# Retention attention beside a swish MoE on one core: pairs of attention chunks replaced by single chunks, one PSUM bank re-labelled

## The chip, the cores and the metric

The kernel runs on one core of a Trainium2 chip. The metric is the device time of one execution in microseconds (us); before the change it was 314.33 us, the median of 3 runs (313.99 to 314.72).

## What is computed

The reference, cut to what matters (8 batches, 8 heads, 576 positions, head size 64; model width 512, hidden width 2048):

```python
scores = scale * np.matmul(q, k.transpose(0, 1, 3, 2))
gamma = 1.0 - 2.0 ** (-5.0 - np.arange(H, dtype=np.float32))
rel = pos[:, None] - pos[None, :]
Dmat = np.where(rel >= 0, gamma[:, None, None] ** rel[None, :, :], 0.0)
attn_out = np.matmul(scores * Dmat[None], v)
x = attn_out.transpose(0, 2, 1, 3).reshape(B * S, H * D)      # 4608 x 512
h = x @ w_in                                                  # 4608 x 2048
out = (h * sigmoid(beta * h)) @ w_out                         # 4608 x 512
```

Since the decay is a power of a position difference, the kernel scales q rows by gamma^i and v rows by gamma^-j, so that the decay mask becomes a plain 0/1 causal mask.

## The kernel before

**The work.** Of each batch, positions 0 to 511 are cut into four chunks of 128 (c = 0 to 3), and the 64 positions left over of two batches make one tail chunk (four in all). The list seq (lines 51 to 55) gives their order; the two tails of four batches stand side by side after batch 3 and after batch 7. For each chunk the kernel does these steps:

- load_q, load_kv, load_tail (lines 73 to 103): loads, issued by SyncE (the SP queue).
- pre_q, pre (lines 232 to 266): GpSimd (POOL) scales q into qs and v into vn and casts k into kn.
- kT and qT, the transposes. For batches 0 to 2 they are done by TensorE (PE) into PSUM (t_q, t_k, lines 284 to 295) and copied out by ScalarE (ACT) or VectorE (DVE). From batch 3 on (XB = 3) they are DMA transposes that ACT issues (x_q, x_k, x_tail, lines 271 to 282).
- a_sc (line 304): 8 matmuls for the scores, each using 64 of the 128 rows of the array (the profile's form 64*128), then DVE multiplies two halves by the mask into R (line 324).
- a_O (line 345): 8 matmuls R times v, each filling 64 of the 128 columns (form 128*64).
- a_cross (line 326): 4 matmuls (8 half-size ones for a tail) that add what earlier chunks of the batch contribute through the running state; full array. Chunk 0 has none.
- a_x (line 362): the chunk's output is copied from PSUM to xT, by DVE for chunks 8 and later.
- a_st (line 375): 4 matmuls that add the chunk to the state; full array; ACT copies the state out in two halves (line 390). Tails have none.

**The order.** The program is written in the order in which each engine runs it (manual schedule). MoE work is a list called fill, of which one element, here called a filler, is four matmuls of 512 columns: up (line 395) makes one of 16 hidden slices of a block of 512 rows, and ACT applies silu from PSUM into gT; down (line 408) makes a quarter of an output tile, and after each fourth one DVE copies it out and SP stores it. Blocks come in the order 0 to 6, tails, 7. Fillers 0 to 15 are up of block 0, 16 to 31 down of block 0, 32 to 51 up of block 1, 52 to 67 down of block 1, 68 to 83 up of block 2, 84 to 99 down of block 2, and so on by 32. Each attention step has a filler number, and merged (line 432) puts it ahead of that filler in the program. So a step's number fixes its place in every engine's queue: PE, DVE, ACT, POOL and SP each work through their own part in order, and wait there for what they need.

Chunks 0 to 3 are done ahead of the fillers (lines 446 to 483). Chunks 4 to 7 have fractional numbers written out by hand (lines 517 to 520). From chunk 8 (E = 8) on, pair_steps (line 534) handles two chunks i and i+1 in two visits, five fillers apart:

```python
def first(i):  a_st(i); a_sc(i); a_sc(i + 1)
def second(i):
    for f in (a_O, lambda j: a_cross(j, False), a_x):
        f(i); f(i + 1)
    a_st(i + 1)
```

Loads, casts and transposes of a pair stand a fixed number of fillers ahead of its first visit. Lines 553 to 563 spread 14 pairs over the blocks.

**Buffers.** PSUM has eight banks here: tag mm 3 (fillers, and the second half of t_q), sc 2 (scores), O 2 (outputs, the scores of the second chunk of a pair, and the PE transposes), st 1 (state). In the on-chip memory there are 4 kn and 4 kT buffers, 6 vn, 6 for loaded k and v, 2 for loaded q; loaded tails share the q buffers.

Of the kernel before, what the change touches and what calls it, by code (L numbers as in the profile page):

```python
# [19 lines left out]
def kernel(  # L20
# [30 lines left out]
    seq = []  # L51
    for b in range(B):
        seq += [(b, c) for c in range(CB)]
        if b % CB == CB - 1:
            seq += [(None, b // 2 - 1), (None, b // 2)]
    full = [i for i, (b, _) in enumerate(seq) if b is not None]

    consts = ctx.enter_context(tc.tile_pool(name="consts", bufs=1))
# [8 lines left out]

    NQ = 6
    E = 2 * CB
    XB = 3  # L70
    q_tiles, kv_tiles = {}, {}

# [23 lines left out]
    def load_tail(t):  # L96
        if t >= NT:
            return
        tl = stage.tile([P, 4, H, D], F32, name="tln", tag="qn", bufs=2)
        for j, src in enumerate((q, k, v)):  # L100
            for x in range(2):
                nc.sync.dma_start(tl[x * TL:(x + 1) * TL, j], src[2 * t + x, :, MB:, :].rearrange("h s d -> s h d"))
        tail_tiles[t] = tl
# [142 lines left out]
    def pre(i):  # L246

        b, c = seq[i]
        vn = sb.tile([P, H, D], BF16, name="vn", tag="vn", bufs=6)
        if b is None:  # L250
            t = tail_tiles.pop(c)
            qk = sb.tile([P, 2, H, D], BF16, name="kn", tag="kn", bufs=4)
            qkT = sb.tile([P, 2, HP, P], BF16, name="kT", tag="kT", bufs=4)
            nc.gpsimd.tensor_tensor(qk[:, 0], t[:, 0], gains(gq, CB), ALU.mult)
            nc.gpsimd.tensor_copy(qk[:, 1], t[:, 1])
            nc.gpsimd.tensor_tensor(vn[:], t[:, 2], gains(gv, CB), ALU.mult)
            live[i] = dict(qk=qk, qkT=qkT, kT=qkT[:, 1], vn=vn)
            return
        if c % 2 == 0:
            pair[b, c // 2] = (sb.tile([P, 2, H, D], BF16, name="kn", tag="kn", bufs=4),  # L260
                               sb.tile([P, 2, HP, P], BF16, name="kT", tag="kT", bufs=4))
        t = kv_tiles.pop(i)
        kn, kT = pair[b, c // 2]
        live[i] = dict(kn=kn[:, c % 2], kT=kT[:, c % 2], vn=vn)
        nc.gpsimd.tensor_copy(kn[:, c % 2], t[:, 0])  # L265
        nc.gpsimd.tensor_tensor(vn[:], t[:, 1], gains(gv, c), ALU.mult)  # L266
# [15 lines left out]
        turn(live[i]["qkT"], live[i]["qk"])  # L282

    def t_q(b, u):
        T = psum.tile([P, CB, 2, P], BF16, name="T", tag="mm" if u else "O", bufs=3 if u else 2)
        for i in range(CB):
            for p in range(2):
                nc.tensor.transpose(T[:, i, p, :], heads(batch[b]["qs"][:, i], 2 * u + p), ident[:])  # L288
        (nc.vector.tensor_copy if u else nc.scalar.copy)(batch[b]["qT"][:, :, 2 * u:2 * u + 2], T[:])

    def t_k(i):
        T = psum.tile([P, HP, P], BF16, name="T", tag="O", bufs=2)
        for p in range(HP):
            nc.tensor.transpose(T[:, p, :], heads(live[i]["kn"], p), ident[:])  # L294
        nc.scalar.copy(live[i]["kT"], T[:])  # L295

# [7 lines left out]
    def a_sc(i):  # L304
        L = live[i]
        L["R"] = R = sb.tile([P, 2, HP, P], BF16, name="R", tag="R", bufs=2)

        tag = "O" if i >= E and (i - E) % 2 else "sc"
        sc = [psum.tile([P, HP, P], F32, name="sc", tag=tag, bufs=2) for _ in range(2)]
        for p in range(HP):  # L310
            for j in range(2):
                r = slice(j * D, (j + 1) * D)
                rhs, view = q_cols(i, r, p)
                nc.tensor.matmul(view(sc[j][:, p, :]), L["kT"][r, p, :], rhs, start=True, stop=True,  # L314
                                 skip_group_check=True)
        mask = causal if seq[i][0] is not None else causal2
        m_b = mask[:].unsqueeze(1).to_broadcast([P, HP, P])
        if i == CB - 1:

            half = sb.tile([P, HP, P], BF16, name="half", tag="half", bufs=1)  # L320
            nc.scalar.copy(half[:], sc[1][:])
            sc[1] = half
        for j in range(2):
            nc.vector.tensor_tensor(R[:, j], sc[j][:], causal4[:] if i == CB - 1 else m_b, ALU.mult)  # L324

    def a_cross(i, first):

        b, c = seq[i]
        L = live[i]
        if first:  # L330
            L["O"] = psum.tile([P, HP, P], F32, name="O", tag="O", bufs=2)
        if c == 0 and b is not None:
            return
        for p in range(HP):
            rhs, view = q_cols(i, slice(0, P), p)
            if b is None:
                for x in range(2):
                    r = slice(x * TL, (x + 1) * TL)
                    nc.tensor.matmul(L["O"][:, p, r], ends[(2 * c + x) % 4][:, p, :], rhs[:, r],  # L339
                                     start=False, stop=True, skip_group_check=True)  # L340
            else:
                nc.tensor.matmul(view(L["O"][:, p, :]), sbds[(c - 1) % NS][:, p, :], rhs,  # L342
                                 start=first and p == 0, stop=not first, skip_group_check=True)

    def a_O(i):

        b, c = seq[i]
        L = live[i]

        early = i < E  # L350
        if not early:
            L["O"] = psum.tile([P, HP, P], F32, name="O", tag="O", bufs=2)
        O, R, vn = L["O"], L["R"], L["vn"]
        crossed = b is None or c > 0
        for j, p in [(n // HP, n % HP) if early else (n % 2, n // 2) for n in range(H)]:
            nc.tensor.matmul(O[j * D:(j + 1) * D, p, :], vn[:, 2 * p + j, :], R[:, j, p, :],  # L356
                             start=p == 0 and not (early and crossed), stop=early or not crossed,
                             skip_group_check=True)
        if early:
            a_x(i)  # L360

    def a_x(i):
        b, c = seq[i]
        O = live[i]["O"]
        if b is None:
            x = xt(B)[:, :, c, :]
        else:
            x, O = xt(b)[:, :, :, c * PC:(c + 1) * PC], O.rearrange("k p (i s) -> k p i s", i=CB)
        if i == CB - 1:
            nc.vector.tensor_copy(x[:, :2], O[:, :2])  # L370
            nc.scalar.copy(x[:, 2:], O[:, 2:])
        else:
            (nc.scalar.copy if i < E else nc.vector.tensor_copy)(x, O[:])  # L373

# [145 lines left out]
               steps(7, d0 + 12, d0 + 15, u1 + 0.8, u1 + 2.7, u1 + 2.8, u1 + 2.9)]  # L520


    def first(i):
        a_st(i)
        a_sc(i)
        a_sc(i + 1)

    def second(i):
        for f in (a_O, lambda j: a_cross(j, False), a_x):
            f(i)  # L530
            f(i + 1)
        a_st(i + 1)

    def pair_steps(i, at, to):
        b, c = seq[i]
        st = [(at, F(first, i)), (to, F(second, i))]
        if b is None:
            return st + [(at - 31, F(load_tail, c)), (at - 21.5, F(pre, i)), (at - 21, F(load_tail, c + 1)),
                         (at - 13, F(pre, i + 1)), (at - 12, F(x_tail, i)), (at - 9.5, F(x_tail, i + 1))]
        n = full.index(i)  # L540
        if b < XB:
            if c == 0:
                st += [(at - 12 + x, F(pre_q, b, x)) for x in range(4)]
                st += [(at - 5.5, F(t_q, b, 0)), (at - 4.5, F(t_q, b, 1))]
                st += [(at - 6.5 + x / 2, F(pre, i + x)) for x in range(CB)]
            return st + [(at - 3.5, F(t_k, i)), (at - 2.5, F(t_k, i + 1))]
        if c == 0:
            st += [(at - 30, F(load_q, b))] + [(at - 20 + x, F(pre_q, b, x)) for x in range(4)]
            st += [(at - 14 + 1.5 * x, F(x_q, b, x)) for x in range(2)]
        return st + [(at - 28, F(load_kv, n)), (at - 26, F(load_kv, n + 1)), (at - 16, F(pre, i)),  # L550
                     (at - 15, F(pre, i + 1)), (at - 10.5, F(x_k, b, c // 2))]

    todo = list(range(E, len(seq), 2))
    for n in range(1, B - 1):

        take = [i for i in todo if seq[i][0] == n + 1 or n == B - 2 or seq[i] == (None, 0) and n == CB - 1]
        todo = todo[len(take):]
        lo, hi = (base[n] + 11, base[n + 1] - 8) if n == 1 else (base[n] + 3, base[n + 1] - 8)
        if len(take) == 2 and n > 1:
            hi -= 6  # L560
        for x, i in enumerate(take):
            at = lo + x * (hi - lo) / (len(take) - 1)
            streams.append(pair_steps(i, at, at + 5))
    assert not todo
    merged(fill, *streams)


# [28 lines left out]
```

## Time and profile before

| | |
|---|---|
| median of 3 runs | 314.33 us (313.99 to 314.72) |
| profiled execution: its own time / its span | 314.33 us / 312.4 us |
| busy: PE, DVE, ACT, POOL | 303.1, 108.7, 141.4, 97.6 us |
| PE idle in 0 to 21.2 us, 21.2 to 66.0 us, after 309 us | 5.35, 0.49, 3.4 us |
| one filler (4 matmuls of 512 columns) back to back | 0.863 us (16 of them: 13.81 us) |
| DMA traffic | 52.79 MB, mean 169 GB/s |

All times inside an execution count from the start of the span. The span runs from the first to the last instruction; the execution's own time is 1.9 us more. A line of the timeline gives start, length, engine, source line, operation, output and inputs, the part of the array (rows*columns) and the number of instructions merged; since each matmul's end is modelled with its latency, the cost of a group is read from its start to the start of the next group.

### The profile page before, as it was taken

The numbers are of one execution on the slowest core, as the hardware profiler recorded it, in microseconds if no ns is written. First come the engines' busy times: TensorE is split into PE (matmuls) and PEld (weight loads), VectorE is DVE, ScalarE is ACT, GpSimd is POOL, SyncE is SP. The second block draws the span as 40 slices with busy tenths as digits, with TensorE's granted clock in tenths as the row PEclk, the third lists the DMA queues.
The fourth block names the chain that finished last, engine by engine and source line by source line (L and its number), as shares of the span: only waits on it lengthen the run. The fifth ranks groups of instructions, "written<-read, shape, count | busy, mean of one in ns | idle before, by whom it ended". The sixth has DMA issues, their size and how long they took to land.

```text
span 312.4 us, 5313 instructions
## 1 busy us (share of the span) xinstructions
PE 303.1 (97%) x2151; PEld 155.8 (50%) x2151; DVE 108.7 (35%) x193; ACT 141.4 (45%) x246; POOL 97.6 (31%) x128
## 2 busy tenths in 40 slices
PE   7689999999999999999999999999999999999995
PEld 5464455554554454545545544445455454444444
DVE  6645465232434051434441334133415420010012
ACT  5467726784237601671067106720574037207700
POOL 3752065936333371453228021912420000000000
PEclk9979999999999999999999999999999999999999
DMA  7999999997999989996999496959942110031012
GB/s 201 221 369 387 378 231 268 221 262 160 161 217 165 229 157 237 183 252 128 176 269 123 104 231 207 198 93 202 193 72 52 67 69 0 14 88 36 0 67 69
DMA packets 123368, 52.79 MB, mean 169 GB/s; under 512 B 105664, under 2 KB 115280, under 8 KB 123344
## 3 DMA queue, kind: packets, MB, share of 16 engines
q1 hardware_dynamic: 97968, 46.15, 61.5%
q10 hardware_dynamic: 25376, 6.30, 15.5%
q8 instruction: 17, 0.28, 0.4%
q14 instruction: 7, 0.06, 0.1%
HBM read 36.71 MB, written 9.44 MB: 148 GB/s over the span
## 4 chain that ended last, share of the span: by engine, by line
PE 92%; SPq 3%; DMA 2%; ACT 1%; DVE 1%; issue 0%; POOL 0%; ACTq 0%
PE ph L402 40%; PE po L415 40%; PE O L356 3%; PE sc L314 3%; SPq L91 2%; PE O L342 2%; PE st L385 2%; DMA kvn<-in_k_dram 2%; PE T L294 1%; PE T L288 1%; DVE R L324 0%; ACT xT L373 0%; PE O L339 0%; DVE ot L422 0%; SPq L80 0%
## 5 line engine op out<-in xcount | busy, mean ns | idle before, releaser
L404 ACT ACTIVATE gT<-ph,beta_sb 128x512 bf16<-128x512 f32 (+2 forms) x148 | 99.0, 676 | 84.4 <-PE ph L402 83.7
L402 PE MATMUL ph<-xT,w_in_sb 128*128 128x512 bf16 (+2 forms) x592 | 129.5, 374 | 1.0 <-DVE xT L370 0.5
L415 PE MATMUL po<-w_out_sb,gT 128*128 128x512 bf16 (+2 forms) x608 | 129.5, 368 | 0.0
L402 PEld LDWEIGHTS <-w_in_sb 128*128 128x128 bf16 x592 | 56.0, 98 | 65.3 <-issue 1.2
L415 PEld LDWEIGHTS <-gT 128*128 128x128 bf16 x608 | 56.9, 98 | 61.8
L324 DVE TENSOR_TENSOR R<-sc,causal 128x512 bf16<-128x512 f32 x71 | 44.4, 683 | 57.7 <-PE sc L314 55.8
L422 DVE COPY ot<-po 128x512 f32<-128x512 f32 (+2 forms) x38 | 25.2, 663 | 89.9 <-PE po L415 89.8
L242 POOL TENSOR_TENSOR qs<-qn,gq 128x512 bf16<-128x512 f32 x26 | 27.4, 1081 | 38.8 <-DMA qn<-in_q_dram 38.8
L266 POOL TENSOR_TENSOR vn<-kvn,gv 128x512 bf16<-128x512 f32 x32 | 33.3, 1042 | 19.6 <-DMA kvn<-in_v_dram 15.1
L265 POOL CAST kn<-kvn 128x512 bf16<-128x512 f32 x32 | 19.5, 609 | 50.1 <-DMA kvn<-in_k_dram 49.5
L373 DVE CAST xT<-O 128x512 bf16<-128x512 f32 x28 | 18.0, 686 | 32.0 <-PE O L356 15.2
L390 ACT CAST sbd<-st 64x256 bf16<-64x256 f32 x48 | 17.5, 364 | 19.8 <-PE st L385 17.5
L390 ACT CAST end<-st 64x256 bf16<-64x256 f32 x16 | 5.8, 365 | 29.5 <-PE st L385 29.3
L385 PE MATMUL st<-vn,kn 128*128 128x128 bf16 x128 | 12.8, 224 | 0.2 <-POOL vn L266 0.2
L356 PE MATMUL O<-R,vn 128*64 128x128 bf16 x288 | 12.7, 227 | 0.0
L356 PEld LDWEIGHTS <-vn 128*64 128x64 bf16 x288 | 9.0, 111 | 6.9 <-issue 6.1
L314 PE MATMUL sc<-qT,kT 64*128 64x128 bf16 x256 | 11.0, 220 | 0.8 <-ACT kT L295 0.6
L385 PEld LDWEIGHTS <-kn 128*128 128x128 bf16 x128 | 9.6, 101 | 4.0 <-issue 0.2
L295 ACT COPY kT<-T 128x512 bf16<-128x512 bf16 x12 | 7.0, 585 | 9.8 <-PE T L294 9.8
L314 PEld LDWEIGHTS <-kT 64*128 64x128 bf16 x288 | 8.3, 95 | 4.7 <-ACT kT L295 2.0
L342 PE MATMUL O<-qT,sbd 128*128 128x128 bf16 x96 | 8.9, 228 | 0.1
L202 PE MATMUL ph<-warm 128*128 128x128 f32 (+1 forms) x22 | 6.8, 455 | 1.3 <-DVE warm L113 1.3
(56 smaller groups left out, 85.3 us busy)
## 6 DMA issues: line engine op xcount, KB each, us to landing
qn<-in_q_dram SPq DMA_DIRECT2D x16, 512.0 KB, 5.5
kvn<-in_k_dram SPq DMA_DIRECT2D x32, 256.0 KB, 5.9
kvn<-in_v_dram SPq DMA_DIRECT2D x32, 256.0 KB, 5.9
out_dram<-ot SPq DMA_DIRECT2D x31, 256.0 KB, 3.3
wt<-in_moe_w_out_dram SPq DMA_DIRECT2D x4, 1024.0 KB, 9.3
wt<-in_moe_w_in_dram SPq DMA_DIRECT2D x3, 1024.0 KB, 11.0
out_dram<-ot SPq DMA_DIRECT2D x9, 128.0 KB, 2.4
wt<-in_moe_w_in_dram SPq DMA_DIRECT2D x2, 512.0 KB, 5.5
```

The costliest lines, as they stand in the source:

```text
L242: e.tensor_tensor(batch[b]["qs"][:, cs, hs], q_tiles[b][:, hs, cs].rearrange("p h i d -> p i h d"), gq[:, cs, hs].unsqueeze(3).to_broadcas ...
L265: nc.gpsimd.tensor_copy(kn[:, c % 2], t[:, 0])
L266: nc.gpsimd.tensor_tensor(vn[:], t[:, 1], gains(gv, c), ALU.mult)
L314: nc.tensor.matmul(view(sc[j][:, p, :]), L["kT"][r, p, :], rhs, start=True, stop=True, skip_group_check=True)
L324: nc.vector.tensor_tensor(R[:, j], sc[j][:], causal4[:] if i == CB - 1 else m_b, ALU.mult)
L356: nc.tensor.matmul(O[j * D:(j + 1) * D, p, :], vn[:, 2 * p + j, :], R[:, j, p, :], start=p == 0 and not (early and crossed), stop=early or ...
L385: nc.tensor.matmul(st[:, p, :], heads(L["kn"], p), heads(L["vn"], p), start=(c == 0 and p == 0), stop=True, skip_group_check=True)
L390: nc.scalar.copy(s[r, :, j * D:(j + 1) * D], st[r, :, j * D:(j + 1) * D])
L402: nc.tensor.matmul(ph, w_in_sb[:, ko, fo * P:(fo + 1) * P], xts[m][:, ko, :, w], start=(ko == 0), stop=(ko == KO - 1))
L404: nc.scalar.activation(gts[m][:, fo, :, w], ph, ACT.Silu, scale=beta_sb[:, fo:fo + 1])
L415: nc.tensor.matmul(po[:, :nn], gT[:, fo, ms, :], w_out_sb[:, fo, n0:n0 + nn], start=(fo == 0), stop=(fo == FO - 1))
L422: nc.vector.tensor_copy(ot, po[:, :nn])
```

## The change

- The two visits of a pair become one visit per chunk (function group): at its number, chunk i gets its scores (a_sc), and right after them chunk i-1 gets a_O with a_cross and a_x, and then its a_st. The 28 chunks from chunk 8 on so take 29 visits (the first has scores alone, the last outputs alone) in place of 28.
- a_x is no function of its own any more; its code is the end of a_O.
- PSUM tag O has 1 bank, and a new tag T has 1 bank, for the PE transposes (t_k and the first half of t_q). Outputs of chunks 1 and 3 go to an mm bank. Scores always go to sc.
- Tails stand alone after batches 3, 4, 6 and 7, and their loads have one buffer of their own.
- kn and kT have 3 buffers in place of 4, vn 5 in place of 6.
- The visits are spread from the first filler of a block (from filler 47 in block 1, as before) to three before its end. All steps tied to a chunk move with it; so do loads, by the new offsets. Filler numbers of some, before and after: load_q of batch 3: 41 and 40; pre_q of batch 3: 51 to 54 and 45 to 48; x_q of batch 3: 57, 59 and 51, 53; x_k of its first pair: 61 and 55; load_q of batch 4: 84 and 68; x_q of batch 4: 100, 101 and 86, 88; x_k of its first pair: 103 and 90; load_q of batch 7: 169 and 164, its x_q: 185, 187 and 182, 184.

The hand-written part for chunks 0 to 7 keeps its order. The diff, cut to its core:

```diff
-        if b % CB == CB - 1:
-            seq += [(None, b // 2 - 1), (None, b // 2)]
+        if b > 2 and b != 5:
+            seq.append((None, (b - 1) // 2 - (b == 3)))
...
-        tl = stage.tile([P, 4, H, D], F32, name="tln", tag="qn", bufs=2)
+        tl = stage.tile([P, 3, H, D], F32, name="tln", tag="tln", bufs=1)
...
-        T = psum.tile([P, CB, 2, P], BF16, name="T", tag="mm" if u else "O", bufs=3 if u else 2)
+        T = psum.tile([P, CB, 2, P], BF16, name="T", tag="T" if u == 0 else "mm", bufs=1 if u == 0 else 3)
...
-        T = psum.tile([P, HP, P], BF16, name="T", tag="O", bufs=2)
+        T = psum.tile([P, HP, P], BF16, name="T", tag="T", bufs=1)
...
-        tag = "O" if i >= E and (i - E) % 2 else "sc"
-        sc = [psum.tile([P, HP, P], F32, name="sc", tag=tag, bufs=2) for _ in range(2)]
+        sc = [psum.tile([P, HP, P], F32, name="sc", tag="sc", bufs=2) for _ in range(2)]
...
-            L["O"] = psum.tile([P, HP, P], F32, name="O", tag="O", bufs=2)
+            tag, bufs = ("mm", 3) if i in (1, 3) else ("O", 1)
+            L["O"] = psum.tile([P, HP, P], F32, name="O", tag=tag, bufs=bufs)
...
-            L["O"] = psum.tile([P, HP, P], F32, name="O", tag="O", bufs=2)
+            L["O"] = psum.tile([P, HP, P], F32, name="O", tag="O", bufs=1)
...
-        if early:
-            a_x(i)
-
-    def a_x(i):
...
+        if not early:
+            a_cross(i, False)
...
-    def pair_steps(i, at, to):
...
+    def group(i, at):
+        st = []
+        if i < len(seq):
+            b, c = seq[i]
+            if b is None:
+                st += [(at - 28, F(load_tail, c)), (at - 14, F(pre, i)), (at - 10, F(x_tail, i))]
+            else:
+                n = full.index(i)
+                if b < XB:
+                    if c == 0:
+                        st += [(at - 12 + x, F(pre_q, b, x)) for x in range(4)]
+                        st += [(at - 5.5, F(t_q, b, 0)), (at - 4.5, F(t_q, b, 1))]
+                        st += [(at - 6.5 + x / 2, F(pre, i + x)) for x in range(CB)]
+                    st += [(at - 2.5, F(t_k, i))]
+                else:
+                    if c == 0:
+                        st += [(at - (25 if b == XB else 32), F(load_q, b))]
+                        st += [(at - 20 + x, F(pre_q, b, x)) for x in range(4)]
+                        st += [(at - 14 + 1.5 * x, F(x_q, b, x)) for x in range(2)]
+                    if c % 2 == 0:
+                        a0, a1 = (24, 22) if b == XB and c == 0 else (29, 26)
+                        st += [(at - a0, F(load_kv, n)), (at - a1, F(load_kv, n + 1)), (at - 16, F(pre, i)),
+                               (at - 15, F(pre, i + 1)), (at - 10.5, F(x_k, b, c // 2))]
+            st += [(at, F(a_sc, i))]
+        if i > E:
+            st += [(at, F(a_O, i - 1)), (at, F(a_st, i - 1))]
+        return st
...
+        need = (seq.index((n + 1, CB - 1)) if n < B - 2 else len(seq) - 1) + 2
+        todo = range(done, need)
+        first = base[n] + (11 if n == 1 else 0)
+        last = base[n + 1] - 3
+        streams += [group(i, first + x * (last - first) / max(1, len(todo) - 1)) for x, i in enumerate(todo)]
```

More of the change, by code (lines that the diff above doesn't have):

```diff
@@ L248, in pre @@
         b, c = seq[i]
-        vn = sb.tile([P, H, D], BF16, name="vn", tag="vn", bufs=6)
+        vn = sb.tile([P, H, D], BF16, name="vn", tag="vn", bufs=5)
         if b is None:
             t = tail_tiles.pop(c)
-            qk = sb.tile([P, 2, H, D], BF16, name="kn", tag="kn", bufs=4)
-            qkT = sb.tile([P, 2, HP, P], BF16, name="kT", tag="kT", bufs=4)
+            qk = sb.tile([P, 2, H, D], BF16, name="kn", tag="kn", bufs=3)
+            qkT = sb.tile([P, 2, HP, P], BF16, name="kT", tag="kT", bufs=3)
             nc.gpsimd.tensor_tensor(qk[:, 0], t[:, 0], gains(gq, CB), ALU.mult)
@@ L259, in pre @@
         if c % 2 == 0:
-            pair[b, c // 2] = (sb.tile([P, 2, H, D], BF16, name="kn", tag="kn", bufs=4),
-                               sb.tile([P, 2, HP, P], BF16, name="kT", tag="kT", bufs=4))
+            pair[b, c // 2] = (sb.tile([P, 2, H, D], BF16, name="kn", tag="kn", bufs=3),
+                               sb.tile([P, 2, HP, P], BF16, name="kT", tag="kT", bufs=3))
         t = kv_tiles.pop(i)
@@ L358, in a_O @@
                              skip_group_check=True)
-        if early:
-            a_x(i)
-    def a_x(i):
-        b, c = seq[i]
-        O = live[i]["O"]
+        if not early:
+            a_cross(i, False)
         if b is None:
@@ L520 @@
                steps(7, d0 + 12, d0 + 15, u1 + 0.8, u1 + 2.7, u1 + 2.8, u1 + 2.9)]
[L523 to L532, printed above, removed]
-    def pair_steps(i, at, to):
[L535 to L551, printed above, removed]
@@ L553 @@
-    todo = list(range(E, len(seq), 2))
-    for n in range(1, B - 1):
[L556 to L563, printed above, removed]
@@ L564 @@
-    assert not todo
+    def group(i, at):
[25 more added lines that the diff above has]
+        return st
@@ L565 @@
+    done = E
+    for n in range(1, B - 1):
+        need = (seq.index((n + 1, CB - 1)) if n < B - 2 else len(seq) - 1) + 2
[3 more added lines that the diff above has]
+        streams += [group(i, first + x * (last - first) / max(1, len(todo) - 1)) for x, i in enumerate(todo)]
+        done = need
     merged(fill, *streams)
```

## Prediction

> **What bounds the kernel now.** I read the page's busy times and slices first, then PE's list of waits, then PE's timeline.
>
> ```profile
> span 312.4 us, 5313 instructions
> PE 303.1 (97%) x2151; PEld 155.8 (50%) x2151; DVE 108.7 (35%) x193; ACT 141.4 (45%) x246; POOL 97.6 (31%) x128
> ...
> PE   7689999999999999999999999999999999999995
> ...
> PEclk9979999999999999999999999999999999999999
> ```
>
> ```profile
> PE ph L402 <- DVE xT L370: 0.5, 1, 0.5
> PE ph L402 <- ACT xT L373: 0.3, 1, 0.3
> ```
>
> The second fence is all that PE waited for between 21.2 us and its last matmul. From then on the time is the sum of what PE issues. So the change can gain little there (only in the first 21 us does PE idle, 5.35 us, and the order there is untouched), and whatever it adds to PE's queue, or makes PE wait for, is paid in full. The third slice has the one dip of the clock; I come back to it.
>
> **Part 1: more changes between kinds of matmul.** PE's timeline of one pair, then of single chunks in the hand-written part:
>
> ```profile
> 106.28 1.89 PE L415 MATMUL po<-w_out_sb,gT 128*128 128x512 bf16 x8
> 108.01 0.39 PE L385 MATMUL st<-vn,kn 128*128 128x128 bf16 x4
> 108.33 0.62 PE L314 MATMUL sc<-qT,kT 64*128 64x128 bf16 x16
> 108.88 4.49 PE L415 MATMUL po<-w_out_sb,gT 128*128 128x512 bf16 x20
> 113.30 0.64 PE L356 MATMUL O<-R,vn 128*64 128x128 bf16 x16
> 113.87 0.62 PE L342 MATMUL O<-qT,sbd 128*128 128x128 bf16 x8
> 114.33 0.39 PE L385 MATMUL st<-vn,kn 128*128 128x128 bf16 x4
> 114.55 7.93 PE L415 MATMUL po<-w_out_sb,gT 128*128 128x512 bf16 x36
> ```
>
> ```profile
> 50.95 0.40 PE L314 MATMUL sc<-qT,kT 64*128 64x128 bf16 x8
> 51.27 0.42 PE L356 MATMUL O<-R,vn 128*64 128x128 bf16 x8
> 51.63 1.04 PE L415 MATMUL po<-w_out_sb,gT 128*128 128x512 bf16 x4
> ```
>
> Read starts against starts. Four st matmuls take 0.22 us before a filler (114.33 to 114.55) but 0.32 before scores (108.01 to 108.33): entering the half-row form costs 0.10. Scores to fillers: 16 take 0.55, 8 take 0.33 (55.47 to 55.80 in the same view), so 8 are 0.22 and leaving costs 0.11. Twenty filler matmuls before O take 4.42, where 20 x 0.216 (8 in 1.73) is 4.32: entering the half-column form costs 0.10. Sixteen O take 0.57, eight 0.36: leaving costs 0.15. Scores straight to O: 0.32 - 0.22 = 0.10.
>
> A pair pays 0.10 + 0.11 + 0.10 + 0.15 = 0.46; 14 pairs 6.4 us. A chunk of the new order (scores, then the previous chunk's O) pays 0.10 + 0.10 + 0.15; over 29 visits: 28 x (0.10 + 0.15) + 27 x 0.10 + 0.11 + 0.10 = 9.9 us. The matmuls themselves are the same in number and shape. **Sum: +3.5 us** (3.0 to 3.8 with the rounding of the rows).
>
> [...]
>
> **Part 2: transposes of batch 3 ahead of their data.** The rows of POOL and ACT around the first DMA transposes:
>
> ```profile
> 73.38 4.04 POOL L242 TENSOR_TENSOR qs<-qn,gq 128x512 bf16<-128x512 f32 x4 [5.59 <-DMA qn<-in_q_dram]
> ...
> 78.80 1.56 ACTq L272 DMA_TRANSPOSE qT<-qs  x1
> ...
> 80.40 0.58 ACT L295 COPY kT<-T 128x512 bf16<-128x512 bf16 x1 [1.10 <-PE T L294]
> 80.48 2.23 ACTq L272 DMA_TRANSPOSE qT<-qs  x1
> ```
>
> POOL scales batch 3's q only from 73.38 on, when its load has landed. That load stands on SP right behind the stores of block 0's down, before and after, so it doesn't come earlier, though its filler number falls from 41 to 40. Of the four scalings (1.01 each), x_q's first half needs two (75.40) and the second all four (77.42). Now x_q stands at fillers 57 and 59, in a down stage where ACT has nothing else; afterwards at 51 and 53. At 51 ACT comes to it behind the silu of filler 50, at about 72.3, and waits 3 us for POOL. Behind it in ACT's queue: the silu of filler 51, the state copies of chunk 8, the second x_q, and the kT copy that chunk 10's scores need at filler 56. PE's way there, from the rows: filler 45 starts 0.23 earlier (one t_k is later), 65.71; visit 47 at 67.44 (0.43); fillers 47, 48; t_k 0.23; fillers 49 to 51; visit 52 at 72.41 (1.00); 52, 53; t_k; 54; filler 55 at 76.23. Its fourth matmul (76.88) needs the silu of filler 51, which starts after 75.45 + 1.56 = 77.0 and takes 0.69. PE waits 0.9 us and ends the filler at 78.0. The second x_q starts at about 77.8; pairs of such issues in this trace end 3.4 to 4.0 us after the first began (78.80 to 82.71; 114.81 to 118.18; 123.45 to 127.49), so 79.05 (at the least length, 1.25) to 79.5; the kT copy of 0.58 follows, and scores start at 80.1 in place of 78.1: 2.0 us. **Sum: +2.9 us**, 2.2 with the shortest issues (1.25 each), 3.5 with these two rows' own lengths; nothing if the wait were taken off by an earlier landing, which no row suggests.
>
> What the stall does to the clock the trace shows once:
>
> ```profile
> 13.00:16.00 3.00, 1.28 (x20) 0.90 (x20) 2.90 (x8) 1.21 (x3) 1.94 (x3) 1.00 1.29 237
> 16.00:17.00 1.00, 0.86 (x14) 0.66 (x12) 0.59 (x1) 0.83 (x2) 0.77 (x1) 0.58 1.09 335
> 17.00:19.00 2.00, 2.00 (x26) 1.44 (x25) 0.54 (x1) 1.33 (x4) 1.36 (x4) 0.50 1.09 359
> 19.00:20.00 1.00, 1.00 (x11) 1.00 (x10) 0.85 (x3) 0.92 (x3) 0.84 (x2) 0.72 1.03 377
> ```
>
> (Columns: stretch, length, busy PE, PEld, DVE, ACT, POOL, granted clock, DMA.) After 3 us with PE 43% busy the clock was near half for 3.4 us: 0.42 + 2 x 0.50 + 0.28 = 1.7 us lost. Around the stall PE works some 0.3 of 3.2 us, less than there, so I take the same **+1.7 us**; the other end is 0.
>
> [...]
>
> **Part 3: what else moves, and what hides it.**
> - Single O bank: the closest visits are three fillers apart (65, 68). After a visit's scores DVE needs 2 x 0.62 for R and 0.69 for xT, done 2.6 us after its start; the next O starts at 1.23 + 2.59 + 0.42 = 4.2. Chunks 4 to 7: xT copied by 52.34, O next written at 52.73. Single T bank: nearest at 45.41, the copy of qT ending at 45.31. Uncovered, each costs the tenths by which it is late: 0, up to 0.1.
> - Other transposes: x_q and x_k of batches 4, 5, 7 go into down stages with load_q 18 fillers (15.5 us) ahead, against 11.4 us for the slowest landing of a q load and 4.0 of scaling; no wait. x_k has 10 fillers and a visit (9.9 us) to land, longest landing in the trace 9.9. In block 3's up stage three transposes go; there 20 filler matmuls took 4.54 in place of 4.42 (125.63, chain of waits): -0.1. Next late there: nothing on ACT.
> - kn, kT, vn with fewer buffers: POOL waits for an earlier state visit, at least two visits old when it gets there. SP: 52.79 MB as before; loads pass stores, whose output tiles have four buffers. 0. If POOL or a load were late by more than the cover, ACT waits in front of silu, and PE after three mm banks (2.6 us).
>
> **Sum.** Own time 314.33 (span 312.4 + 1.9), which is also the median: + 3.5 + 2.9 + 1.7 - 0.1 = **322.3 us**.
>
> **Rivals.**
> - [...]
> - *The stall doesn't come*: x_q finds its data: 314.33 + 3.5 - 0.1 = 317.7. For it: only one place is involved, and a landing 3 us earlier removes it. Against: POOL's row says it waited for that DMA, and SP's order ahead of it is the same.
> - *Queues late in later blocks too*: DMA engines are mostly over 90% busy to 210 us, and bursts (q, a tail, three k and v) now stand together: each late batch costs up to 3 us; 325 or more.
> - *Faster*: the dip at 16 to 20 us goes. Place: PE's waits between 13 and 16 us; price: 1.7 us and up to 1.7 of idle there; it decides if the separate T and O banks release t_k of chunks 2 and 3 earlier. With the changes of form free as well, 311 us. Against: those t_k are shown waiting for POOL's kn (13.34, 15.73), not for a bank, and the 3.5 us come from rows.
>
> **Numbers.** Forecast 0.50; no dip 0.20; no stall 0.18; later queues 0.06; faster 0.03; cancelling to within 0.2% (about what a measurement of this kernel can tell from no change) 0.03. Slower is then 0.94. The range: 317.3 (part 1 at its low end, nothing else) to 324.0 (3.8 + 3.5 + 1.7 and 0.7 for a late queue); outside lie faster, same and most of the later queues, about 0.12.
>
> **What would show it.** Right: more time in sc, O and cross rows from start to start, as priced; the first transpose of ACT at 75.4 in place of 78.8, a PE wait of some 0.9 us on silu near 77 and of 2 us on the kT copy near 78 to 80; a clock near 0.5 in a stretch of 3.4 us after it; no PE wait behind that. Wrong: PE rows behind 60 us with waits elsewhere, above all on silu in up stages; single visits that cost no more than halves of pairs; or POOL's scaling of batch 3 well ahead of 73 us.

## The result and the profile after

The changed kernel took 319.38 us (median of 4 runs, 318.45 to 320.35) against 314.33 us of the kernel before (313.99 to 314.72): a ratio of 1.016, 95% interval 1.0128 to 1.0193, or 5.0 us more. The profiled execution took 319.29 us, with a span of 317.5 us.

The page of the changed kernel: the busy times, and the granted clock in 40 slices of 7.9 us.

```profile
PE 306.9 (97%) x2151; PEld 155.6 (49%) x2151; DVE 108.5 (34%) x193; ACT 142.1 (45%) x246; POOL 97.1 (31%) x128
...
PEclk9969999999999999999999999999999999999999
```

PE has the same 2151 matmul records and is busy 3.8 us longer. The clock still dips in the third slice only. PE's list of waits has just one place behind 61 us; here it stands in PE's timeline, with the rows of POOL and ACT that lead to it:

```profile
72.89 4.04 POOL L243 TENSOR_TENSOR qs<-qn,gq 128x512 bf16<-128x512 f32 x4 [4.75 <-DMA qn<-in_q_dram]
74.97 1.33 ACTq L273 DMA_TRANSPOSE qT<-qs  x1
76.34 0.69 ACT L400 ACTIVATE gT<-ph,beta_sb 128x512 bf16<-128x512 f32 x1 [3.08 <-DVE xT L369]
76.97 1.32 ACTq L273 DMA_TRANSPOSE qT<-qs  x1
78.33 0.59 ACT L296 COPY kT<-T 128x512 bf16<-128x512 bf16 x1 [0.66 <-PE po L411]
78.97 0.40 PE L313 MATMUL sc<-qT,kT 64*128 64x128 bf16 x8 [0.89 <-ACT kT L296]
```

This is the stall that the prediction described, link by link: POOL waits for the load of q (4.75 us), ACT stands in front of the first transpose until POOL has done two of its four scalings (half of the 4.04 us is over at 74.91), the kT copy stands behind the second, and PE's scores wait for that copy. It is 0.89 us long, not 2.9, and the silu of filler 51 (76.34) does not hold PE at all. Behind it, PE's timeline of one single visit:

```profile
84.73 0.40 PE L313 MATMUL sc<-qT,kT 64*128 64x128 bf16 x8
85.06 0.41 PE L356 MATMUL O<-R,vn 128*64 128x128 bf16 x8
85.41 0.40 PE L342 MATMUL O<-qT,sbd 128*128 128x128 bf16 x4
85.64 0.39 PE L381 MATMUL st<-vn,kn 128*128 128x128 bf16 x4
85.86 3.62 PE L411 MATMUL po<-w_out_sb,gT 128*128 128x512 bf16 x16
```

From start to start: scores 0.33, O 0.35, cross 0.23, state 0.22. Of the 0.33, eight score matmuls are 0.22 and the change to O 0.11; the 0.35 hold the change from O to the full array. These are the prices of part 1. What PE does in these tenths no run shows: the runs below price a change of form, they don't look inside it.

**Where the 5.1 us of span come from.** The first MoE matmul starts at 22.02 us where it started at 21.20: +0.82. The stall: +0.89. From DVE's last copy (313.94; 309.00 before) to the end of the span: 3.56 in place of 3.4, +0.16. The rest is **+3.2 us**, spread over the 29 visits. It is best read from a stretch that leaves both ends of the span out: from the first scores of chunk 4 (46.60 before, 47.41 after) to DVE's last copy it takes 262.40 and 266.53 us; 4.13 less the stall of 0.89 is 3.24. I call this the steady stretch below. Its ends, before and after:

```profile
46.60 0.40 PE L314 MATMUL sc<-qT,kT 64*128 64x128 bf16 x8
309.00 0.29 DVE L422 COPY ot<-po 128x128 f32<-128x128 f32 x1 [0.60 <-PE po L415]
```

```profile
47.41 0.40 PE L313 MATMUL sc<-qT,kT 64*128 64x128 bf16 x8
313.94 0.29 DVE L418 COPY ot<-po 128x128 f32<-128x128 f32 x1 [0.60 <-PE po L411]
```

The +0.82 comes from a part of the program whose order the change left alone (only its PSUM banks have other labels). The stretches of the changed kernel there (stretch, length, busy PE, PEld, DVE, ACT, POOL, granted clock, DMA share, GB/s):

```profile
15.00:16.00 1.00, 0.30 (x4) 0.30 (x4) 0.96 (x4) 0.00 (x0) 0.61 (x1) 0.53 1.04 257
16.00:21.00 5.00, 5.00 (x51) 3.84 (x51) 2.08 (x4) 3.71 (x8) 3.47 (x8) 0.50 1.07 367
```

The column before the last two is the clock. It is at half from about 15.06 (0.53 in that slice: 0.94 us at half) to about 21.9 us (0.55 in the slice from 21 to 22, 1.00 from there on): 6.8 us, where the kernel before had 3.4 us (16.16 to 19.56). It is a matter of this execution: two of the four runs of the changed kernel, 318.45 and 319.46 us, have a mean granted clock of 1.000 and 0.999, the profiled one 0.989.

### The profile page after: what moved, and what is told of

The parts are those of the page before. It is cut to its first block, busy times and chain, and to the rows that moved or that the text cites. A ratio compares the mean times of both kernels' runs of the same rounds, so it can differ in the third digit from the quotient of the medians.

```text
span 317.5 us, 5319 instructions
## 1 busy us (share of the span) xinstructions
PE 306.9 (97%) x2151; PEld 155.6 (49%) x2151; DVE 108.5 (34%) x193; ACT 142.1 (45%) x246; POOL 97.1 (31%) x128
## 3 DMA queue, kind: packets, MB, share of 16 engines
q1 hardware_dynamic: 97968, 46.15, 60.9%
## 4 chain that ended last, share of the span: by engine, by line
PE 92%; SPq 3%; DMA 2%; ACT 1%; DVE 1%; issue 0%; POOL 0%; ACTq 0%
PE ph L398 39%; PE po L411 39%; PE O L356 4%; PE sc L313 3%; SPq L92 2%; PE st L381 2%; PE O L342 2%; DMA kvn<-in_k_dram 2%; PE T L295 1%; PE T L289 1%; PE O L339 0%; DVE R L323 0%; ACT xT L369 0%; DVE ot L418 0%; PE ph L203 0%
## 5 line engine op out<-in xcount | busy, mean ns | idle before, releaser
L323 DVE TENSOR_TENSOR R<-sc,causal 128x512 bf16<-128x512 f32 x71 | 45.6, 684 | 68.9 <-PE sc L313 66.9
L369 DVE CAST xT<-O 128x512 bf16<-128x512 f32 x28 | 19.1, 681 | 0.9 <-PE O L339 0.9
L356 PE MATMUL O<-R,vn 128*64 128x128 bf16 x288 | 15.7, 232 | 0.0
L313 PE MATMUL sc<-qT,kT 64*128 64x128 bf16 x256 | 13.1, 221 | 1.7 <-ACT kT L296 1.5
L342 PE MATMUL O<-qT,sbd 128*128 128x128 bf16 x96 | 9.9, 229 | 0.0
L381 PEld LDWEIGHTS <-kn 128*128 128x128 bf16 x128 | 8.9, 101 | 1.7 <-issue 0.2
```

The source lines that it names most:

```text
L381: nc.tensor.matmul(st[:, p, :], heads(L["kn"], p), heads(L["vn"], p), start=(c == 0 and p == 0), stop=True, skip_group_check=True)
```

## The experiments

Three theories had to be told apart. **F**: the changes between forms of matmul cost what the rows of single visits say, 3.3 to 3.5 us in all. **Q**: the stall in front of chunk 10's scores hangs on the landing of q for batch 3, so its length is what PE arrives too early by. **C**: the clock's dip in the first stage hangs on PE's idle time ahead of it. The rival to F is that the loss is all stall and clock.

### e1: the load of q for batch 3 earlier (changed kernel)

```diff
-                        st += [(at - (25 if b == XB else 32), F(load_q, b))]
+                        st += [(at - (38 if b == XB else 32), F(load_q, b))]
```

> The changed kernel with one number changed: batch 3's q is loaded at filler 27 in place of 40, ahead of four stores on SP. Theory Q (PE's 0.89 us wait at 78.97 us comes from ACT standing at a transpose until POOL has scaled q, and POOL from the load landing at 72.9): POOL's scaling starts near 67.7, right behind its cast of chunk 11, the first transpose starts at once near 73.3, PE waits nowhere behind 61 us, and the time falls by 0.9 us or somewhat more to 317.5 to 318.5 (more in executions in which PE reaches this place earlier). Rival (the two issues of 1.3 us each hold ACT whenever they stand at fillers 51 and 53): the wait stays between 0.5 and 0.9 us and the time at 319.4.

Measured: 317.55 us (316.64 to 319.44, 8 runs), ratio to before 1.0099 (1.0065 to 1.0133). Its timeline has POOL's scaling of that q here:

```profile
70.54 4.04 POOL L243 TENSOR_TENSOR qs<-qn,gq 128x512 bf16<-128x512 f32 x4 [3.54 <-DMA qn<-in_q_dram]
```

POOL scales 2.35 us earlier, and the scores of chunk 10 start at 76.61 with no wait of PE shown in their row. Theory Q holds for the wait, and the rival (a wait of 0.5 to 0.9) is out, though POOL was expected at 67.7 and still waits 3.54 us for the load. The median is 1.8 us below that of the changed kernel, and still 1% above before. Not all of the 1.8 is the load's: the steady stretch takes 265.76 us, 0.77 less than in the changed kernel and 3.4 more than before, and the first stage had no dip of the clock in this profile (first MoE matmul at 19.82).

### e2: the second visit of a pair chunk by chunk (kernel before)

```diff
-        for f in (a_O, lambda j: a_cross(j, False), a_x):
-            f(i)
-            f(i + 1)
+        for x in (i, i + 1):
+            a_O(x)
+            a_cross(x, False)
+            a_x(x)
```

> The kernel before with one thing changed: in the second visit of a pair the outputs and the cross terms go chunk by chunk (8 O, cross, 8 O, cross) in place of 16 O, then both cross terms. Nothing else moves, the matmuls are the same. Theory F (each change of form has a price: leaving the half-column form 0.15, entering it 0.10): 14 pairs x 0.25 = +3.5 us, so 317.8. Rival (single chunks cost more for other reasons: visits, DVE, banks, loads): within 0.5 us of before, 314.3 to 314.8.

Measured: 316.08 us (315.56 to 317.35, 12 runs) against 314.41 of the kernel before run beside it, ratio 1.0046 (1.0021 to 1.0071): +1.67 us. The size that I had expected, 3.5, was a slip of counting: in a pair that begins a batch the first chunk has no cross, so its order doesn't change. Only 8 of the 14 pairs change (six with c = 2 and 3, and two of tails): 8 x 0.25 = 2.0. A pair that does:

```profile
86.22 0.41 PE L356 MATMUL O<-R,vn 128*64 128x128 bf16 x8
86.57 0.40 PE L342 MATMUL O<-qT,sbd 128*128 128x128 bf16 x4
86.89 0.41 PE L356 MATMUL O<-R,vn 128*64 128x128 bf16 x8
...
87.70 1.67 PE L415 MATMUL po<-w_out_sb,gT 128*128 128x512 bf16 x6
```

That is 1.48 us from the first O to the filler; the same pair in the kernel before takes 1.26 (86.62 to 87.88). So 0.22 for one more return to the half-column form, 1.8 for eight. The steady stretch takes 264.49 us, 2.1 more than before, and 0.23 of it is a wait of PE for ACT's silu that before did not have. F holds, and the rival (within 0.5 us of before) is out.

### e3: outputs and state one filler ahead of the scores (changed kernel)

```diff
-            st += [(at, F(a_O, i - 1)), (at, F(a_st, i - 1))]
+            st += [(at - 1, F(a_O, i - 1)), (at - 1, F(a_st, i - 1))]
```

> The changed kernel with outputs and state of a chunk one filler ahead of the next chunk's scores, in place of right behind them. Theory F: half rows straight to half columns (0.10) become leaving half rows (0.11) and entering half columns (0.10), 27 x 0.11 = +3.0 us, so 322.4. Rival (the price hangs on the number of matmuls of a form in a row or on the first visit alone, not on changes): 319.4 within 0.5. A wait of O for R on DVE at the closest visits could add up to 0.5.

Measured: 320.2 us (319.74 to 320.4, 5 runs), ratio to before 1.0171 (1.0134 to 1.0208): only 0.8 above the changed kernel. The total hides two things that went the other way: the first MoE matmul started at 21.04, not 22.02, and the wait in front of chunk 10's scores was 0.27, not 0.89: PE came at 78.10, as in the changed kernel (78.08), but POOL's scaling of q began at 72.27, not 72.89. The steady stretch, net of that one wait, takes 268.51 against 265.64 us: the matmuls cost 2.9 us more. The rows say 27 x 0.11 = 3.0. The miss of the total taught me to compare over this stretch and net of the wait.

### e7: the state between two groups of scores (kernel before)

```diff
     def first(i):
-        a_st(i)
         a_sc(i)
+        a_st(i)
         a_sc(i + 1)
```

> The kernel before, with one thing changed: in the first visit of a pair the state of the first chunk stands between the two groups of scores, not behind both. By the rows of before each of the 12 pairs that have a state then leaves and enters the scores' form once more: 12 x 0.21 = 2.5 us, so 316.9 us under theory F. If the order of forms costs nothing, 314.4.

Measured: 316.79 us (316.1 to 318.14, 6 runs) against 314.46 of the kernel before run beside it, ratio 1.0076 (1.0054 to 1.0097): +2.33 us, or 0.19 for each of 12 pairs, where the rows said 0.21; the steady stretch takes 265.22 us, 2.8 more, of which 0.22 is a new wait for silu. One of the pairs:

```profile
109.99 0.40 PE L314 MATMUL sc<-qT,kT 64*128 64x128 bf16 x8
110.32 0.40 PE L385 MATMUL st<-vn,kn 128*128 128x128 bf16 x4
110.65 0.40 PE L314 MATMUL sc<-qT,kT 64*128 64x128 bf16 x8
110.98 1.25 PE L415 MATMUL po<-w_out_sb,gT 128*128 128x512 bf16 x5
```

From the first scores to the filler that is 0.99 us, with the scores' form entered once more ahead of it (about 0.10, filler to scores); the same groups of the prediction's pair take 0.87 (108.01 to 108.88), so 0.22 less. Nothing but the order of three groups differs, and no matmul was added. F holds for the half-row form too. By their medians e2 and e7 put 0.21 and 0.19 us on leaving a form and coming back.

### e4: extra matmuls through the dip (kernel before)

```diff
     a_cross(1, True)
+    warm_up(2, 128)
     t_k(2)
     a_st(1)
+    warm_up(2, 128)
     a_sc(2)
     pre(3)
+    warm_up(4, 128)
     t_k(3)
```

The eight added matmuls write to a buffer that nothing reads. (The expectations call them filler matmuls; they are no part of the fillers of the MoE.)

> The kernel before with eight further filler matmuls in float32 where PE stands idle between 13 and 15.7 us (two ahead of the transposes of chunk 2, two ahead of its scores, four ahead of the transposes of chunk 3). Theory C (the clock falls to half at 16.2 us since PE was idle more than half of the 3.4 us before): the clock stays at 1.00 in 16 to 20 us, the first MoE matmul starts 1.0 to 1.7 us earlier than 21.2, and the time falls by up to as much, to 312.6 to 313.5, less if the loads of chunks 4 to 7 or of batch 3 then bind. Rival (the dip does not hang on PE's idleness, or the path at 21 us goes through loads and POOL): 314.3.

Measured: 313.83 us (313.45 to 314.51, 12 runs), ratio to before 0.998 (0.996 to 0.9999). The stretch ahead of the former dip:

```profile
13.00:16.00 3.00, 2.97 (x36) 2.41 (x34) 2.90 (x8) 1.21 (x3) 1.88 (x3) 1.00 1.24 244
```

PE is busy 2.97 of the 3 us between 13 and 16 (1.28 before), the clock stays at 1.00, and the first MoE matmul starts at 20.26, 0.94 earlier. All 12 runs have a mean granted clock of 0.999 or 1.000, against 10 of the 25 runs of the kernel before beside them. So with PE kept busy there the clock stayed up in all 12, as C has it. The median gains 0.6 (314.41 for the kernel before, run beside it), less than the 0.8 to 1.7 expected, and only 0.2 against the median of those ten runs (314.02). Where the rest went is in PE's timeline, behind the first 16 MoE matmuls:

```profile
20.26 3.84 PE L402 MATMUL ph<-xT,w_in_sb 128*128 128x512 bf16 x16 [0.54 <-DVE xT L370]
24.31 10.44 PE L402 MATMUL ph<-xT,w_in_sb 128*128 128x512 bf16 x46 [0.21 <-DVE w_in_sb L180]
```

An earlier start meets the weights, which DVE still casts: 16 matmuls take 4.05 us from start to start, where 16 x 0.216 is 3.46. The kernel before has no such wait (64 matmuls in one row from 21.20 on). Of the 0.94 us, 0.44 are left at the scores of chunk 4 (46.16 for 46.60). It is the best version that the experiments led to; against the kernel before the interval ends at 0.9999.

### e6a and e6: the same extra matmuls in the changed kernel, without and with the early load

The edit of e4, alone (e6a) and together with that of e1 (e6).

> The changed kernel with eight more filler matmuls between 13 and 16 us, which keep TensorE busy through the stretch in which the clock dropped. They should start the first MoE matmul at about 20.3 us in place of 22.02. Theory Q (the stall at chunk 10's scores is tied to the landing of q for batch 3, so an earlier TensorE only waits longer there): the wait grows from 0.9 to 2 to 2.6 us and the time stays at 319.0 to 319.5 us, against 319.4 for the changed kernel. Rival (the 0.9 us is a fixed price that moves with TensorE): the wait stays near 0.9 and the time falls by 0.8 to 1.7 us, to 317.7 to 318.6.

> The changed kernel with the same eight filler matmuls, and with the load of q for batch 3 issued 13 fillers earlier. With the first-stage clock drop and the stall both gone, theory F (what remains is the price of the form changes, 3.3 to 3.5 us) gives the time of the kernel before with the same filler, 313.8, plus 3.3 to 3.5: 317.1 to 317.3 us. If the form changes cost nothing and the loss was all stall and clock, it is 313.8 to 314.3.

Measured: e6a 318.49 us (318.11 to 320.28, 6 runs), e6 316.78 us (316.34 to 317.12, 6 runs); ratios to before 1.0136 (1.0111 to 1.0162) and 1.0071 (1.0054 to 1.0089).

By its total e6a fell to the rival of Q, 0.9 below the changed kernel. Its trace says otherwise. The first MoE matmul started at 19.68, 2.34 us ahead of the changed kernel, and then:

```profile
78.72 0.40 PE L313 MATMUL sc<-qT,kT 64*128 64x128 bf16 x8 [1.48 <-ACT kT L296]
```

The scores of chunk 10 start at 78.72, where the changed kernel had 78.97. Of the lead of 2.34 us, 1.26 are left at the scores of chunk 4 (46.15 for 47.41), since PE meets the weights as in e4, and 0.25 at those of chunk 10, since PE's wait there grew from 0.89 to 1.48 (and PE lost some 0.4 in smaller waits ahead of it). POOL's scaling, behind its wait for the load, begins at 72.65 here and at 72.89 in the changed kernel, though PE came 2.34 us earlier out of the first stage. Behind these scores both kernels take 234.97 to 234.98 us to DVE's last copy. So Q's mechanism holds in the trace, while its two numbers (a wait of 2 to 2.6, a time of 319.0 to 319.5) missed. Of the 0.9 us by which the medians differ the trace accounts for 0.25; another 0.46 lies behind DVE's last copy (3.10 and 3.56 us to the end of the span). The four runs of the changed kernel lie 1.9 us apart, and I leave that part open.

In e6 the wait is 0.42. Against e4, which has the same extra matmuls, the medians differ by 2.95 us, and the steady stretches, net of the wait, by 3.4 (265.65 against 262.29). F had said 3.3 to 3.5 for the medians, so it missed there by 0.35. The rival to F, 313.8 to 314.3, is out: with the dip gone and the stall at 0.42, the new order still costs some 3 us.

### e5b: both transposes of q at filler 51 (changed kernel)

```diff
-                        st += [(at - 14 + 1.5 * x, F(x_q, b, x)) for x in range(2)]
+                        st += [(at - 14 + (0 if b == XB else 1.5 * x), F(x_q, b, x)) for x in range(2)]
```

This edit brings about the stall that the prediction feared.

> The changed kernel with the second transpose of q of batch 3 issued at filler 51 with the first, so that the silu of filler 51 stands behind both. TensorE should wait about 1.3 us for that silu and about 1 us for the copy of k behind it: 2.4 us in all in place of 0.9, and 320.9 us. If a stall of that size also drops the clock, as the prediction held, the clock shows 0.5 for about 3.4 us between 78 and 86 us and the time is about 322.6. If it does not, the clock stays at 1.0 behind 25 us.

Measured: 322.77 us (321.19 to 324.25, 4 runs), ratio to before 1.0261 (1.0229 to 1.0294). PE's two waits in the timeline, then the stretch in which the clock falls:

```profile
78.94 0.51 PE L411 MATMUL po<-w_out_sb,gT 128*128 128x512 bf16 x1 [2.63 <-ACT gT L400]
...
80.19 0.60 PE L313 MATMUL sc<-qT,kT 64*128 64x128 bf16 x8 [0.74 <-ACT kT L296]
```

```profile
79.00:80.00 1.00, 0.46 (x1) 0.03 (x1) 0.41 (x1) 0.95 (x3) 0.82 (x1) 0.54 1.33 247
```

PE waits 2.63 us for the silu and 0.74 for kT (I had expected 1.3 and 1; the two transposes took 3.41 us together, and PE, with no dip in the first stage of this execution, came at 76.31). Then the clock is at half from about 79.08 to 85.90 (1.00 up to 79, 0.54 as shown, 0.50 from 80 to 85, 0.55 from 85 to 86, 1.00 behind): 6.8 us. The eight scores that took 0.40 elsewhere take 0.60 here. All four runs have a mean granted clock of 0.984 to 0.989, against three of the 17 runs of the changed kernel, e1 and e3. So behind a stall of this size the clock did drop, as the prediction held for the change itself, and the drop cost more than its 1.7. Worked out: the steady stretch takes 272.01 us, 6.4 more than the changed kernel's net of its wait; the two waits are 3.37 of them, and the other 3.0 are what 6.8 us at half clock cost a PE that is nearly always busy. That the median met the 322.6 of the expectation is luck: the waits and the drop were both longer than expected, and the first stage was shorter.

## Why the prediction was right or wrong

- **What bounds the kernel**: right. PE has one wait behind 61 us, and what the change adds to PE's queue is paid in full.
- **Part 1, +3.5 us**: right, in mechanism and size. The steady stretch gives +3.2, with the -0.1 of part 3 in it. e2, e3 and e7 show that changes of form have this price, with no other edit beside it, by rows and by the steady stretch less its waits: 2.0 and 1.9, 3.0 and 2.9, 2.5 and 2.6. By their medians e2 and e7 give 1.7 and 2.3.
- **Part 2, the stall, +2.9 us**: right in its place and its chain, mis-sized; it measured 0.89. Two steps failed. First, the step by which ACT would be done: I held that the load of q doesn't come earlier, but POOL's scaling began at 72.89, not 73.38, so the first transpose started at 74.97 where I put 75.4; the two took 1.33 and 1.32 where I put 1.56 and up to 1.7, and so the silu of filler 51 began at 76.34, not 77.0. PE's wait of 0.9 for that silu fell away, and with it the late start of the second transpose; the scores stood at 78.97, not 80.1. Second, PE's arrival: 78.08 (78.97 less 0.89), not 77.2, because the first stage took 0.82 longer in this execution. 1.1 and 0.9 make up the 2.0. In e6a, where PE came at 77.24, only the first error is left: 1.48 us. The 0.82 and the 0.89 are not independent: while q's landing sets when chunk 10's scores start, a PE that comes later only waits less.
- **The clock behind the stall, +1.7 us**: 0 in this kernel. The step that failed is "PE works some 0.3 of 3.2 us": it rested on the stall of 2.9. Around a wait of 0.89 or 1.48 us the clock stayed at 1.00 in one profile each; around 2.63 and 0.74 us close together (e5b) it fell, though no single gap there was over 2.63, and cost 3.0. No dip, to which the prediction gave a chance of 0.20, is what came; with the stall of 2.9 kept, its sum would be 314.33 + 3.5 + 2.9 - 0.1 = 320.6, where 319.38 was measured.
- **Part 3**: right as far as seen. PE waits for no bank, no cast and no load behind 61 us but at the one place. DVE's R takes 0.68 to 0.69 us (56 of them behind 66 us) where I put 0.62, well inside the cover.
- **Not foreseen, +0.82 us**: the first stage. I wrote that its order is untouched, which is so, and took its time as fixed, which it isn't: see the table in the last section.
- **Sum.** Against the predicted 8.0 us, the profiled execution lost 5.0: 3.2 for forms, 0.89 for the stall, 0.82 for the first stage, and some tenths at the end. Direction and main term were right; the two terms around the stall were too large by 3.7 us, and the unforeseen one took back 0.8, which is luck. That 319.4 still lies inside the range owes much to the width of the range: it reached from part 1 alone to the full stall with its dip.

## What to carry to other kernels

Here, with TensorE busy 97% of the span, the order of its matmul groups had a price of its own, 0.10 to 0.15 us by the rows for entering or leaving a form: keep groups of one form side by side, read the price of a change start to start, and count the changes group by group (e2's expectation failed on pairs that have no cross). Here ACT came to a transfer ahead of its data and held the silu and the copy queued behind it; what that costs is the difference of two arrival times, so a stall hung on a load can eat what was gained ahead of it (e6a: 0.25 of 2.34 us were left behind it), and an earlier load is the cheap remedy (e1: no wait of PE shown at that place). Compare traces stage by stage before totals: here a stage whose order no edit touched moved by as much as the effects in question (0.82 us, beside a stall of 0.89), and half of an earlier start of the MoE was lost again behind it (e4: 0.44 of 0.94 us were left).

## What the runs showed of the hardware that was not expected

The clock drops that the profiles show here are about 3.4 us long (before, e2, e3) or twice that (the changed kernel, e7, e5b). In the ten profiles of this case the first stage shows no stretch at half clock, one of about 3.4 us, or one of about 6.8 us, and the start of the first MoE matmul follows it:

| stretch at half clock between 15 and 22 us | first MoE matmul starts (us) |
|---|---|
| none, as first written: e1, e5b | 19.82, 19.91 |
| none, with the extra matmuls: e4, e6, e6a | 20.26, 20.17, 19.68 |
| about 3.4 us: before, e2, e3 | 21.20, 20.80, 21.04 |
| about 6.8 us: the changed kernel, e7 | 22.02, 22.07 |

All kernels but e4, e6 and e6a run nearly the same code up to there, and both codes, the one before and the changed one, met dips of different length; so the length of the dip belonged to the execution, not to the kernel. Nor did PE's busy share alone decide it: in those seven profiles PE is busy 1.28 to 1.55 of the 3 us from 13 to 16, and 1.39 both in e3, with a dip, and in e5b, without. So the step of the prediction from 43% busy to half clock names one of several outcomes; only with the extra matmuls (2.97 to 3.00 of the 3 us) do all profiles, three, come without a dip, and 22 of the 24 runs of those kernels have a mean granted clock of 0.999 or 1.000.

The dips may also explain part of the spread of 313.64 to 317.79 us in the 25 runs of the kernel before beside e1 to e4: ten with a mean granted clock of 0.999 or 1.000 have a median of 314.02 us, eleven at 0.995 (the value of the profile with one stretch of 3.4 us) one of 314.37, and the two at 0.983 and 0.984 took 317.79 and 317.39. Where in those executions the clock fell is not recorded. The half-clock stretch of e5b has the same length as the longer ones of the table, 6.8 us.

What sets these lengths, and where in an execution such a stretch begins, no run shows.
